# Filler matmuls ahead of and behind the PV of heads 25 to 27, and the tail rows in other loads

## The chip, the cores and the metric

The kernel runs on one core of a Trainium2 chip. The metric is device time in microseconds, from the start to the end of one execution; each run is one execution, and the median over runs is compared. All data are float32.

## What is computed

One decode step for a batch of 2, with one query position. The input x (2 x 512) is normalised over its 512 features, and the result goes to two branches that are added to x:

```
xn  = layernorm(x)                             # no scale, no shift
q   = xn @ wq                                  # 32 heads of 128
p   = softmax(q . k[:, :, -2048:] / sqrt(128)) # per head, over the last 2048 cached positions
att = (p @ v[:, :, -2048:]) @ wo               # 32 * 128 -> 512
glu = ((xn @ w_gate) * (xn @ w_up)) @ w_down   # 512 -> 1376 -> 512, no nonlinearity
y   = x + att + glu
```

Keys and values of the window are 2 x 32 x 2048 x 128 floats each, 134 MB of the 159.57 MB that are loaded. Each of them is used once.

## The kernel before

The inputs are laid out anew beforehand as one long `stream`, in the order in which they are used, so that a load of `n` columns is 128 rows of `n` consecutive floats. `blocks` lists the loads and the fields in each; `packed` fills loads of 15872 columns (7936 KB). There are three such buffers, the tiles named `step`. `pump` issues the next load on SyncE's queue (SP) when the last field of a buffer has been used (`done`); SP takes its issues in order.

For a head h the work is this. `products` (VectorE) multiplies the keys by the query in place, `sums` adds over the 128 features, `maxima` takes the maximum (with a reduction over the partitions on GpSimd), `weights` the exponentials (ScalarE) and their sum, `reciprocals` one over the sum. `pv` multiplies the weights by the values on TensorE into a PSUM tile `o_ps` and copies it out on ScalarE; `transpose` turns the result into columns `oT`, scaled by the reciprocals; `project_o` multiplies by the head's rows of wo and adds into `acc`. The order on TensorE, VectorE, ScalarE and SP is the order in which the program is written (`InOrder`).

A head's PV is eight matmuls (`weigh`), each of 16 stationary columns and 512 moving ones. A float32 matmul stands in the trace as two instructions, called halves below. PV runs some heads behind the products. After head 28's step the ends are written out by hand: products of heads 28, 29 and 30, then PV of heads 25 to 27 (`pv([H - 7]), pv([H - 6, H - 5])`), their transposes and output projections, PV of 28, and so on to head 31. Between these stand filler matmuls, `keep_busy(n)`: they multiply a constant by n columns of `spare_in` into a PSUM tile `spare` that nothing reads.

The values of head 25 lie in two loads: the first half (four matmuls) with the keys of heads 28 and 29, the second half with the keys of 30 and the values of 26 and 27. The next load holds the keys of 31, the values of 28 and two blocks of w_down.

The last 96 rows of w_down (1376 = 10 * 128 + 96) don't fill a block of 128. 46 of them lie, beside x itself, in the field `wr` of the stream; the last 50 lie as 25 rows of two side by side in `tail`, and are loaded into rows 28 to 52 of the tile `wd_tail`, five rows at a time, behind the first four loads. The rows of `wd_tail` below 28 are zero. `down_rest` multiplies both by the GLU's hidden values (`hX`), early on, at head 3.

## Time and profile before

| | |
|---|---|
| median of 3 runs | 379.49 us (379.06 to 384.83) |
| the profiled execution | 379.92 us, span 378.1 us |
| TensorE, VectorE, ScalarE busy | 257.4, 295.4, 57.2 us |
| loaded from HBM | 159.50 MB, 422 GB/s over the span |
| DMA queue of SP | 97.8% of 16 engines' span |

The span runs from the first to the last instruction of the profiled execution; its time is 1.8 us longer. The times in rows of the trace are microseconds from the span's start. All instructions of the wrapped engines stand under line 126, the wrapper's, so rows are told apart by tiles: `o_ps` is PV, `tr` the transposes, `acc` the output projections and w_down, and `q` is the queries' projection or, late in the program, the fillers, whose tile comes from the same pool.

### The profile page before, as it was taken

The numbers are of one execution on the slowest core, as the hardware profiler recorded it, in microseconds if no ns is written. First come the engines' busy times: TensorE is split into PE (matmuls) and PEld (weight loads), VectorE is DVE, ScalarE is ACT, GpSimd is POOL, SyncE is SP. The second block draws the span as 40 slices with busy tenths as digits, with TensorE's granted clock in tenths as the row PEclk, the third lists the DMA queues.
The fourth block names the chain that finished last, engine by engine and source line by source line (L and its number), as shares of the span: only waits on it lengthen the run. The fifth ranks groups of instructions, "written<-read, shape, count | busy, mean of one in ns | idle before, by whom it ended". The sixth has DMA issues, their size and how long they took to land.

```text
span 378.1 us, 2875 instructions
## 1 busy us (share of the span) xinstructions
PE 257.4 (68%) x1096; PEld 88.2 (23%) x1096; DVE 295.4 (78%) x145; ACT 57.2 (15%) x260; POOL 25.2 (7%) x74
## 2 busy tenths in 40 slices
PE   3166796886587880776668806895647774738996
PEld 3132123222222220222123202331212221202343
DVE  4069998369979479999179999892899999999550
ACT  1002011110211210021012002111101110202131
POOL 1000000000001000000000000000000000000010
PEclk9999696798576896598958865889567888666999
DMA  8999999999999999999999999999999999999993
GB/s 341 435 488 436 416 404 434 437 430 432 431 437 430 430 430 432 450 437 430 443 432 431 430 430 437 437 426 437 430 430 430 432 443 430 437 426 417 420 424 121
DMA packets 3950, 159.73 MB, mean 422 GB/s; under 512 B 457, under 2 KB 713, under 8 KB 994
## 3 DMA queue, kind: packets, MB, share of 16 engines
q1 hardware_dynamic: 3938, 159.57, 97.8%
q8 instruction: 8, 0.13, 0.1%
q14 instruction: 4, 0.03, 0.0%
HBM read 159.50 MB, written 0.07 MB: 422 GB/s over the span
## 4 chain that ended last, share of the span: by engine, by line
DMA 61%; DVE 19%; PE 17%; ACT 1%; issue 0%; SPq 0%; DVEq 0%
DMA step<-in_stream_dram 61%; DVE s L126 9%; DVE step L126 9%; PE o_ps L126 6%; PE acc L126 4%; PE q L126 4%; PE tr L126 3%; ACT o_sb L126 1%; ACT oT L126 0%; DVE m L126 0%; SPq L126 0%; DVE o_out L126 0%; DVE rec L126 0%; DVEq L126 0%
## 5 line engine op out<-in xcount | busy, mean ns | idle before, releaser
L126 DVE TENSOR_TENSOR step<-step,q 128x4096 f32<-128x4096 f32 x31 | 136.8, 4412 | 45.8 <-DMA step<-in_stream_dram 42.0
L126 DVE TENSOR_REDUCE s<-step 128x32 f32<-128x4096 f32 x32 | 141.4, 4419 | 1.1
L126 PE MATMUL o_ps<-step,p 128*16 128x512 f32 x512 | 81.5, 693 | 50.0 <-DMA step<-in_stream_dram 49.9
L126 PE MATMUL q<-step,xnb 128*128 128x512 f32 (+1 forms) x128 | 77.2, 754 | 31.7 <-DMA step<-in_stream_dram 31.7
L126 PEld LDWEIGHTS q<-step,xnb 128*128 128x128 f32 x128 | 29.5, 246 | 83.2 <-issue 67.8
L126 PE MATMUL acc<-step,oT 128*2 128x512 f32 (+1 forms) x88 | 38.3, 597 | 8.5 <-ACT oT L126 8.5
L126 PE MATMUL tr<-first,o_sb 128*128 128x2 f32 (+4 forms) x192 | 29.8, 274 | 15.7 <-ACT o_sb L126 11.8
L126 PEld LDWEIGHTS o_ps<-step,p 128*16 128x16 f32 x512 | 14.3, 103 | 106.1 <-DMA step<-in_stream_dram 58.6
L126 PEld LDWEIGHTS tr<-first,o_sb 128*128 128x128 f32 (+2 forms) x192 | 27.1, 216 | 40.4 <-ACT o_sb L126 34.3
L126 ACT COPY o_sb<-o_ps 128x512 f32<-128x512 f32 x23 | 13.5, 585 | 150.2 <-PE o_ps L126 150.2
L321 POOL PARTITION_ALL_REDUCE mm<-m x32 | 11.4, 357 | 241.1 <-DVE rec L126 136.0
L126 ACT ACTIVATE nm<-mm 128x2 f32<-128x2 f32 x32 | 6.6, 205 | 126.7 <-POOL mm L321 126.7
L337 POOL PARTITION_ALL_REDUCE sum<-rs x32 | 12.7, 398 | 99.9 <-ACT p L126 99.9
L126 ACT ACTIVATE p<-s,nm 128x16 f32<-128x16 f32 x64 | 19.2, 300 | 1.0
L126 PE MATMUL o_ps<-step,xn 128*2 128x512 f32 (+1 forms) x48 | 14.9, 682 | 5.9 <-DMA step<-in_stream_dram 5.9
L126 ACT ACTIVATE oT<-tr,rec 128x1 f32<-128x1 f32 x64 | 12.1, 260 | 27.7 <-PE tr L126 27.7
L126 DVE TENSOR_TENSOR step<-step,tr 128x4096 f32<-128x4096 f32 x1 | 4.4, 4422 | 15.0 <-DMA step<-in_stream_dram 15.0
L126 ACT ACTIVATION_READ_ACCUMULATOR p<-s,nm 128x1 f32 x64 | 11.9, 187 | 0.0
L126 PEld LDWEIGHTS acc<-step,oT 128*2 128x2 f32 x88 | 4.3, 88 | 21.8 <-ACT oT L126 12.2
L126 DVE RECIPROCAL rec<-sum 128x2 f32<-128x2 f32 x32 | 5.0, 155 | 4.2 <-POOL sum L337 4.2
L126 PE MATMUL q<-xnb,mean_w 128*128 128x512 f32 (+4 forms) x20 | 7.4, 461 | 0.0
L126 PE MATMUL acc<-step,hT 128*2 128x128 f32 (+2 forms) x72 | 7.1, 310 | 0.0
(40 smaller groups left out, 39.2 us busy)
## 6 DMA issues: line engine op xcount, KB each, us to landing
step<-in_stream_dram SPq DMA_DIRECT2D x15, 7936.0 KB, 31.8
step<-in_stream_dram SPq DMA_DIRECT2D x1, 7808.0 KB, 38.8
step<-in_stream_dram SPq DMA_DIRECT2D x1, 7680.0 KB, 20.9
step<-in_stream_dram SPq DMA_DIRECT2D x1, 7552.0 KB, 57.9
step<-in_stream_dram SPq DMA_DIRECT2D x1, 4864.0 KB
step<-in_stream_dram SPq DMA_DIRECT2D x1, 3328.0 KB, 20.0
step<-in_stream_dram SPq DMA_DIRECT2D x1, 2304.0 KB, 25.0
step<-in_stream_dram SPq DMA_DIRECT2D x2, 1024.0 KB, 14.2
```

Of the source, the lines that this page charges most:

```text
L126: made = call(*args, **kwargs)
L321: nc.gpsimd.partition_all_reduce(mm, m, P, bass_isa.ReduceOp.max)
L337: nc.gpsimd.partition_all_reduce(sum_t[h], rs, P, bass_isa.ReduceOp.add)
```

## The change

It has three parts. First, three matmuls of 512 columns go ahead of the PV of heads 25 to 27. Like the other fillers they write `spare`; their moving operand is head 29's keys after `products` has multiplied them. They stand in the program between `products` and `sums` of head 29. Second, the one filler of 512 columns behind the output projections of 25 to 27 becomes three, of 512, 512 and 256. Third, the 25 rows of `tail` come in one load, and the last four of the 46 rows leave `wr` for a new input `edge`; they are loaded one by one into rows 24 to 27 of `wd_tail`, first 512 columns. The stream keeps its size: `wr` holds zeros where they were.

```diff
-NT, FT, FP, TS = 2, 25, 28, 5
+NT, FT, FP, TS = 2, 25, 28, 4
...
-    for i in range(0, FT, FT // TS):
-        sp.dma_start(wd_tail[FP + i : FP + i + FT // TS, :], tail[i : i + FT // TS, :])
+    sp.dma_start(wd_tail[FP : FP + FT, :], tail)
+    for i in range(TS):
+        sp.dma_start(wd_tail[FP - TS + i : FP - TS + i + 1, :D], edge[i : i + 1, :])
...
+    spare = ps_q.tile([P, B, GC], F32, name="q")[:, 0, :]
     for h in (H - 4, H - 3):
         products(h)
+        if h == H - 3:
+            for i in range(3):
+                pe.matmul(
+                    spare, mean_w, got["k", h][0][:, i * FB : (i + 1) * FB], start=True, stop=True
+                )
         sums(h)
         maxima(h)
         weights(h)
         reciprocals(h - 1)
 
     h = H - 2
-    spare = ps_q.tile([P, B, GC], F32, name="q")[:, 0, :]
     products(h)
     sums(h)
     o_sbs = pv([H - 7]), pv([H - 6, H - 5])
...
     for i in range(H - 7, HF):
         project_o(i)
-    keep_busy(GC)
+    for n in (GC, GC, 256):
+        keep_busy(n)
...
-    mixed[:, :RX] = np.concatenate([a, rest[:FX]]).reshape(RX, 2, HD).swapaxes(0, 1)
+    whole = np.concatenate([a, rest[: FX - TS]])
+    mixed[:, : RX - TS] = whole.reshape(RX - TS, 2, HD).swapaxes(0, 1)
...
         "tail": rest[FX:].reshape(NT, FT, D).swapaxes(0, 1).reshape(FT, NT * D),
+        "edge": rest[FX - TS : FX],
```

TensorE's program at the new fillers, between the output projections of heads 23 and 24 (`acc`) and PV of head 25 (`o_ps_93` with the weights `p_97`) and head 26 (`o_ps_92`, `p_98`):

```order
 L126 MATMUL acc<-step,oT_111 2x512
 L126 MATMUL acc<-step,oT_108 2x512
+L126 MATMUL q<-step,mean_w 128x512 x3
 L126 MATMUL o_ps_93<-step,p_97 16x512 x8
 L126 MATMUL o_ps_92<-step,p_98 16x512 x8
```

All eight matmuls of head 25, of both halves of its values, now stand behind the three fillers.

TensorE's program between the output projections of 26 and 27 and PV of head 28 (`p_100`), which two blocks of w_down (`hT`) follow:

```order
 L126 MATMUL acc<-step,oT_110 2x512
 L126 MATMUL acc<-step,oT_111 2x512
-L126 MATMUL q<-xnb,mean_w 128x512
+L126 MATMUL q<-xnb,mean_w 128x512 x2
+L126 MATMUL q<-xnb,mean_w 128x256
 L126 MATMUL o_ps_93<-step,p_100 16x512 x8
 L126 MATMUL acc<-step,hT 2x512 x2
```

One filler has become two of its size and one of half.

SP's queue at the start of the program:

```order
 L126 DMA step<-in_stream_dram 128x15104
-L126 DMA wd_tail<-in_tail_dram 5x1024 x5
+L126 DMA wd_tail<-in_tail_dram 25x1024
+L126 DMA wd_tail<-in_edge_dram 1x512 x4
 L126 DMA step<-in_stream_dram 128x15872 x15
 L126 DMA step<-in_stream_dram 128x9728
```

Five small issues stay five, at the same place behind the first three large loads.

## The prediction

> **What bounds the kernel now.** First the page: span, engines, DMA, and the chain that ended last.

> ```profile
> span 378.1 us, 2875 instructions
> PE 257.4 (68%) x1096; PEld 88.2 (23%) x1096; DVE 295.4 (78%) x145; ACT 57.2 (15%) x260; POOL 25.2 (7%) x74
> q1 hardware_dynamic: 3938, 159.57, 97.8%
> DMA 61%; DVE 19%; PE 17%; ACT 1%; issue 0%; SPq 0%; DVEq 0%
> ```

> The loads fill the 16 DMA engines for 97.8% of the span, so up to the last loads the kernel runs at the pace of its stream. The edit on TensorE sits at the end of that stream, so the chain in order of time comes next (start, length, what).

> ```profile
> 303.27 37.99 DMA step<-in_stream_dram
> ...
> 341.31 7.20 PE o_ps L126 x40
> 348.51 1.00 PE tr L126 x8
> ...
> 351.05 0.54 PE q L126 x2
> 351.58 2.67 PE acc L126 x6
> 354.25 1.06 PE q L126 x2
> 355.31 1.84 PE o_ps L126 x16
> ...
> 362.83 1.84 PE o_ps L126 x16
> ...
> 366.76 0.98 PE o_ps L126 x8
> ...
> 368.38 1.84 PE o_ps L126 x16
> 370.21 0.52 PE q L126 x2
> 370.74 1.02 PE o_ps L126 x8
> ...
> 373.48 1.92 PE acc L126 x80
> ```

> From 341.31 to 375.4 us the chain is TensorE's own program, one piece after the other. It starts when the load with the values of heads 26 and 27 lands, and no later load stands in it. The page's list of issues says how far behind the loads are (KB, median us to landing), and the queue's timeline when the first was issued:

> ```profile
> step<-in_stream_dram SPq DMA_DIRECT2D x1, 3328.0 KB, 20.0
> step<-in_stream_dram SPq DMA_DIRECT2D x1, 2304.0 KB, 25.0
> 340.65 15.38 SPq L126 DMA_DIRECT2D step<-in_stream_dram  x6
> ```

> Issued at 340.65, the 3328 KB (values of head 29) land at 360.7, and PV of 29 starts at 362.83: 2.2 us of slack. The 2304 KB (values of 30), issued right behind, land at 366 and are used at 368.38. So the end moves one for one with TensorE, earlier by at most some 2 us, later without limit.

> Last the granted clock (the column after POOL) in stretches of 3.41 us, which fall on the steps of the clock:

> ```profile
> 329.76:333.17 3.41, 3.41 (x11) 0.57 (x10) 3.38 (x4) 0.83 (x5) 0.35 (x1) 0.50 0.99 428
> 333.17:336.58 3.41, 0.69 (x2) 0.00 (x0) 3.38 (x2) 0.06 (x1) 0.40 (x1) 1.00 1.07 465
> 336.58:340.00 3.42, 0.00 (x0) 0.00 (x0) 3.42 (x1) 0.00 (x0) 0.00 (x0) 0.50 0.83 359
> 340.00:343.41 3.41, 2.10 (x12) 0.48 (x16) 2.97 (x4) 1.03 (x6) 0.75 (x2) 0.50 1.03 445
> 343.41:346.82 3.41, 3.41 (x20) 0.67 (x16) 3.38 (x2) 0.45 (x1) 0.00 (x0) 0.50 0.95 411
> 346.82:350.24 3.42, 2.92 (x27) 1.43 (x19) 3.38 (x2) 1.00 (x3) 0.00 (x0) 1.00 1.01 430
> ```

> A stretch in which PE was busy throughout (3.41) is followed by clock 1.00; one with 2.10 or less is followed by 0.50. So 5.5 of the 7.2 us of PV of 25 to 27 run at half clock. That is what the new fillers go for.

> **The change, part by part.** *Fillers ahead.* TensorE takes its instructions in order, and what stands at this place before is:

> ```profile
> 330.80 1.90 PE L126 MATMUL o_ps<-step,p 128*16 128x512 f32 x6
> 332.50 1.36 PE L126 MATMUL o_ps<-step,p 128*16 128x512 f32 x2
> 331.74 4.40 DVE L126 TENSOR_TENSOR step<-step,q 128x4096 f32<-128x4096 f32 x1
> 336.17 4.42 DVE L126 TENSOR_REDUCE s<-step 128x32 f32<-128x4096 f32 x1
> ```

> The eight halves at 330.80 to 333.86 are the first four matmuls of head 25, whose first half of values is there early (an f32 matmul stands as two instructions). They run in idle time today. The fillers stand ahead of them and read head 29's products, which VectorE ends at 336.1. So those eight are now queued behind the fillers: the path gets 3 fillers and 8 halves in front of the 40.

> What a 512 wide matmul with 128 stationary columns takes cold is bounded by the first row, two of them; warm it is the chain's 1.06:

> ```profile
> 153.71 3.75 PE L126 MATMUL q<-step,xnb 128*128 128x512 f32 x4 [11.71 <-DMA step<-in_stream_dram]
> ```

> That is 1.88 cold. With this execution's clock steps: the fillers start at 336.2 on a cold clock, since the work that raised it at 333.17 (the eight halves) no longer stands there. 336.2 to 340.0 holds 3.8 / 1.88 = 2.02 of them. The stretch from 336.58 to 340.00 is then full, so the clock rises at 340.0, and the other 0.98 take 1.04: fillers done at 341.04, just before the load lands. Eight warm halves (the 0.98 of 366.76) end at 342.0, forty (2.5 times the 1.84 of sixteen) at 346.6. Before, the forty ended at 348.51: **1.9 us gained**, and without a rise of the clock there is no gain at all.

> The steps may lie elsewhere against the program in another execution. The earliest rise is 3.41 after 336.2, at 339.6: 1.81 fillers by then, 1.19 x 1.06 more, 0.98 and 4.6 end at 346.4. The latest, where the fillers just miss a step and need the next whole stretch, is 336.2 + 2 x 3.41 = 343.0: all fillers cold (5.64, to 341.84), 1.16 us of the eight at half speed, 0.4 more, 4.6: 348.0. So the gain is between 0.5 and 2.1 against this execution.

> [...]

> *Fillers behind.* One of 512 columns becomes two of 512 and one of 256. 512 cost 1.06 (354.25) and 256 cost 0.54 (351.05), all warm: **1.60 us added**, between the output projections of 25 to 27 and PV of 28. Does a wait cover them? PV of 28 needs the load with head 31's keys; VectorE shows when that comes:

> ```profile
> 352.82 4.42 DVE L126 TENSOR_TENSOR step<-step,q 128x4096 f32<-128x4096 f32 x1 [2.37 <-DMA step<-in_stream_dram]
> 358.95 0.68 DVE L126 COPY o_sb<-acc 2x512 f32<-2x512 f32 x1 [1.71 <-PE acc L126]
> ```

> It lands at 352.8. The projections, 1.9 earlier, end at 352.35; PV of 28 could start at 352.8 without any filler. The fillers (1.06 + 1.06 + 0.54 = 2.66) push it to 355.0 instead of 355.31. So of the 1.9 about 0.3 stays: **the sum is 378.1 - 0.3 = 377.8 of span**. VectorE's copy of the accumulator waits for TensorE (1.71 idle), so it and the sums of head 31 behind it move along with PE; below that idle time VectorE gives no new bound. Over the clock's positions the net is 1.6 - 2.1 = -0.5 to 1.6 - 0.5 = +1.1.

> *The late load.* Head 29's keys and the first half of 25's values share a buffer (they stand in one load). Its next load was issued at 340.65 when the sums of 29 ended; now it waits for the eight halves at 342.0, at most 343.4. It queues behind the load that lands at 352.8, so 10 us cover it. Cost nothing; without that cover 1.4.

> *The tail rows.* Five loads of 5 rows become one of 25, then four of one 2 KB row; five issues stay five:

> ```profile
> wd_tail<-in_tail_dram SPq DMA_DIRECT2D x5, 20.0 KB
> DMA packets 91, 1.69 MB, mean 483 GB/s; under 512 B 41, under 2 KB 41, under 8 KB 66
> ```

> The second row is the DMA view of 57 to 60.5 us: 25 packets of 4 KB (66 - 41), amid a stream that keeps its rate. The same 25 rows move; new are 8 KB. At one engine's share of the page's 422 GB/s (26.4) they are 0.3 us if one engine takes them all. Below nothing is possible too, since one completion takes the place of five, 0.3 the other way. The far bound is a row that costs a whole small transfer, issue to landing, each in turn; the store at the end is the nearest:

> ```profile
> SPq L675 <- DMA out_dram<-o_out: 0.9, 1, 0.9
> 375.74 0.35 SPq L126 DMA_DIRECT2D out_dram<-o_out  x1
> ```

> 0.35 + 0.9 = 1.3, four of them 5 us. I take 0.3, nearest to how the 25 packets ran, and it costs nothing: TensorE now reaches the second half of head 25 at 342.0, 0.7 after its load, PV of 28 stands 2.2 after its own.

> [...] The packets' count agrees with whole rows; which engine takes them no row here shows.

> Against the median: the profiled execution took 379.92, the median of the runs shown is 379.49. 379.92 - 0.3 is 379.6 for the same clock steps; the middle of -0.5 and +1.1 is +0.3, 380.2. Brought to the median (0.43 lower) these are 379.2 and 379.8. **I forecast 379.5 us, no change.**

> **The rivals.**

> *The fillers don't raise the clock before 346.8* (slower). Place: PV of 25 to 27. Price: fillers to 341.84, then 48 halves, 5.6 warm; 5.0 us at half speed do 2.5, the other 3.1 end at 349.9. That is 1.4 late, and 1.6 of fillers behind: +3.0, 382.5 from the median. The net turns into a loss from a rise at 340.7 on (PV of 27 done at 346.9, 1.6 earlier); this case begins past 343.0, the latest rise that full stretches allow. For it: the stretch with 2.10 busy raised nothing, so a gap would do. Against: the fillers and the eight halves leave no gap.

> *The clock is still high when the fillers start* (faster). Then they take 3.2, to 339.4, the eight halves run before the landing, and the forty end at 345.9: 2.6 - 1.6 = 1.0 gained, 378.5. Against: 0.69 busy in 333.17:336.58 let it fall, and there is less there now.

> *The single rows hold one engine for 5 us.* Every load behind is late by it: PV of 26 starts at 346.3 instead of about 342, so the end is some 4 us late, 383.4. Against: 25 packets took their place amid the stream.

> **How the numbers follow.** Forecast 0.74, slow clock 0.12, warm start 0.06, single rows 0.04; 0.04 for what I don't see. The range is 378.4 to 381.6: from the warm start to the late rise with the runs' own scatter of 0.4, and part of the way to the slow clock. About 2% (7.6 us) is what a measurement of this kernel can tell from no change. No case reaches it: faster 0.02, within 0.94, slower 0.04.

> **What would show it.** Three fillers from 336.2 for 4.6 to 5.7 us, clock 1.00 by 343.0 instead of 346.8, PV of 25 to 27 done between 346.4 and 348.0, PV of 28 within 1 us of 355.3, and the queue's late issue at 342 with no hole in the stream. The forecast is wrong if PV of 28 waits for its load behind the fillers, if the clock stays at 0.50 to 346, or if the chain from 350 on holds a DMA step.

## The result, and the profile after

The changed kernel takes 379.19 us (median of 14 runs, 378.06 to 380.18), the kernel before 379.37 in the 14 runs beside it. The ratio is 1.0001, interval 0.999 to 1.0012: no change, as forecast. Executions more than 1.5% above the fastest of their kernel, such as the one of 384.83 us, are left out of this ratio and of those below. The profiled execution took 379.05 us, its span is 377.2.

The chain in order of time (start, length, what), at the place of the edit:

```profile
335.55 5.46 PE q L126 x6
341.01 5.33 PE o_ps L126 x48
346.34 1.00 PE tr L126 x8
...
349.42 2.67 PE acc L126 x6
352.08 2.35 PE q L126 x6
354.43 1.84 PE o_ps L126 x16
...
361.95 1.84 PE o_ps L126 x16
...
372.60 1.92 PE acc L126 x80
```

Three fillers (six halves), then 48 halves of PV where 40 stood, ended at 346.34 instead of 348.51. Behind the projections three fillers stand in 2.35 us where one stood in 1.06. The granted clock (column after POOL), on this execution's steps:

```profile
334.28:337.69 3.41, 2.14 (x3) 1.14 (x4) 3.38 (x2) 0.00 (x0) 0.00 (x0) 0.50 1.03 447
337.69:341.11 3.42, 3.42 (x8) 0.86 (x11) 2.99 (x4) 0.44 (x3) 0.36 (x1) 0.50 0.74 317
341.11:344.52 3.41, 3.41 (x36) 0.83 (x32) 3.41 (x1) 1.04 (x5) 0.40 (x1) 1.00 1.19 514
344.52:347.93 3.41, 2.91 (x29) 1.33 (x21) 3.38 (x2) 1.00 (x3) 0.00 (x0) 1.00 0.90 381
```

The first stretch that the fillers fill is 337.69 to 341.11, and the clock rises at 341.11, as PV starts (341.01). VectorE and the queue of loads:

```profile
340.54 4.42 DVE L126 TENSOR_TENSOR step<-step,q 128x4096 f32<-128x4096 f32 x1 [0.39 <-DMA step<-in_stream_dram]
342.12 0.81 SPq L126 DMA_DIRECT2D step<-in_stream_dram  x2
```

The first row is the product of head 30, which starts as the load with the values of 26 and 27 lands: 340.5, against 341.3 before. The second is the late load, issued at 342.12 behind the eight halves instead of at 340.65; it lands 17.7 us later, at 359.9, where before it was 360.6, and PV of 29 starts behind that, at 361.95. PV of 28 starts 0.88 earlier than before in this pair of profiles. Some 0.7 of it goes with the stream, which is early here: the load above by 0.75, and the products of head 29, which the fillers wait for, by 0.74 (331.00 against 331.74).

### The profile page after: what moved, and what is told of

It reads as the page before. It is cut to its first block, busy times and chain, and to the rows that moved or that the text cites. A ratio compares the mean times of both kernels' runs of the same rounds, so it can differ in the third digit from the quotient of the medians.

```text
span 377.2 us, 2895 instructions
## 1 busy us (share of the span) xinstructions
PE 257.0 (68%) x1106; PEld 89.0 (24%) x1106; DVE 295.4 (78%) x145; ACT 57.4 (15%) x260; POOL 25.3 (7%) x74
## 2 busy tenths in 40 slices
DMA packets 3938, 159.74 MB, mean 423 GB/s; under 512 B 441, under 2 KB 697, under 8 KB 982
## 4 chain that ended last, share of the span: by engine, by line
DMA 60%; PE 20%; DVE 18%; ACT 1%; issue 1%; SPq 0%; DVEq 0%
DMA step<-in_stream_dram 60%; DVE step L126 9%; DVE s L126 8%; PE q L126 7%; PE o_ps L126 6%; PE acc L126 4%; PE tr L126 3%; ACT o_sb L126 1%; ACT oT L126 0%; DVE m L126 0%; SPq L126 0%; DVE o_out L126 0%; DVE rec L126 0%; DVEq L126 0%
## 5 line engine op out<-in xcount | busy, mean ns | idle before, releaser
L126 DVE TENSOR_TENSOR step<-step,q 128x4096 f32<-128x4096 f32 x31 | 136.8, 4412 | 44.3 <-DMA step<-in_stream_dram 38.4
L126 DVE TENSOR_REDUCE s<-step 128x32 f32<-128x4096 f32 x32 | 141.4, 4419 | 1.1
L126 PE MATMUL o_ps<-step,p 128*16 128x512 f32 x512 | 77.3, 663 | 42.7 <-DMA step<-in_stream_dram 42.7
L126 PE MATMUL q<-step,xnb 128*128 128x512 f32 (+1 forms) x128 | 76.2, 742 | 33.6 <-DMA step<-in_stream_dram 33.6
L126 PEld LDWEIGHTS q<-step,xnb 128*128 128x128 f32 x128 | 28.9, 242 | 84.1 <-issue 68.6
L126 PE MATMUL acc<-step,oT 128*2 128x512 f32 (+1 forms) x88 | 36.3, 572 | 8.6 <-ACT oT L126 8.6
L126 PE MATMUL tr<-first,o_sb 128*128 128x2 f32 (+4 forms) x192 | 29.3, 271 | 16.9 <-ACT o_sb L126 11.8
L126 PEld LDWEIGHTS tr<-first,o_sb 128*128 128x128 f32 (+2 forms) x192 | 26.7, 213 | 42.4 <-ACT o_sb L126 35.2
L126 ACT COPY o_sb<-o_ps 128x512 f32<-128x512 f32 x23 | 13.5, 586 | 149.3 <-PE o_ps L126 149.3
L126 PEld LDWEIGHTS o_ps<-step,p 128*16 128x16 f32 x512 | 13.6, 100 | 95.3 <-DMA step<-in_stream_dram 50.1
L126 ACT ACTIVATE nm<-mm 128x2 f32<-128x2 f32 x32 | 6.6, 205 | 125.9 <-POOL mm L323 125.9
L126 ACT ACTIVATE p<-s,nm 128x16 f32<-128x16 f32 x64 | 19.2, 300 | 1.0
L126 PE MATMUL o_ps<-step,xn 128*2 128x512 f32 (+1 forms) x48 | 13.7, 630 | 5.4 <-DMA step<-in_stream_dram 5.4
L126 ACT ACTIVATE oT<-tr,rec 128x1 f32<-128x1 f32 x64 | 12.1, 260 | 27.7 <-PE tr L126 27.7
L126 DVE TENSOR_TENSOR step<-step,tr 128x4096 f32<-128x4096 f32 x1 | 4.4, 4421 | 15.0 <-DMA step<-in_stream_dram 15.0
L126 ACT ACTIVATION_READ_ACCUMULATOR p<-s,nm 128x1 f32 x64 | 11.9, 186 | 0.0
L126 PEld LDWEIGHTS acc<-step,oT 128*2 128x2 f32 x88 | 4.2, 86 | 20.7 <-ACT oT L126 12.1
L126 DVE RECIPROCAL rec<-sum 128x2 f32<-128x2 f32 x32 | 5.0, 155 | 4.9 <-POOL sum L339 4.9
L126 PE MATMUL q<-xnb,mean_w 128*128 128x512 f32 (+4 forms) x24 | 8.7, 465 | 0.0
L126 PE MATMUL q<-step,mean_w 128*128 128x512 f32 x6 | 5.5, 1083 | 4.3 <-DVE step L126 4.3
## 6 DMA issues: line engine op xcount, KB each, us to landing
step<-in_stream_dram SPq DMA_DIRECT2D x1, 3328.0 KB, 17.7
step<-in_stream_dram SPq DMA_DIRECT2D x1, 2304.0 KB, 22.8
```

Of the source, the lines that this page charges most:

```text
L126: made = call(*args, **kwargs)
```

## The experiments

Differences in microseconds below are a ratio times 379.4; the interval stands behind. None of them reaches 2%; they are read from the intervals, over 5 to 12 executions of each kernel. Each profile shows one execution, and the executions differ, as will be seen; the medians decide.

**Fillers ahead alone.** The first part of the change in the kernel before, nothing else.

> The kernel before with the three fillers ahead of PV of 25 to 27 alone; one filler of 512 behind and the tail loads as before. Theory (the fillers ahead raise the clock and shorten PV, the fillers behind give it back, the loads do nothing): PV of 25 to 27 ends 1.4 to 1.9 us sooner after its load, nothing gives that back, PV of 28 starts at 353.4 to 353.9 instead of 355.3, and the median is 1.3 us lower than before (0.5 to 2.1 over the positions of the clock's steps). Rival 1 (the end is set by the stream, so nothing on TensorE counts here): within 0.3 of before. Rival 2 (the single-row loads are what changed the trace): within 0.3 of before.

Measured: 378.22, ratio 0.9965 (0.9948 to 0.9981), so 1.3 us lower (0.7 to 2.0). Its profiled execution was the slowest of its twelve, and shows one way in which they differ. The chain:

```profile
336.38 4.34 PE q L126 x6
340.72 5.27 PE o_ps L126 x48
...
349.07 4.36 PE acc L126 x6
353.43 1.06 PE q L126 x2
354.49 1.84 PE o_ps L126 x16
```

PV ends at 345.99, 2.5 earlier than before, though its load landed at about the same time (341.4): more than the 1.4 to 1.9 expected. But then the projections take 4.36 instead of 2.67: the clock has fallen again behind the transposes, and PV of 28 starts at 354.49, later than the 353.4 to 353.9 expected. More on that below. The clock's stretches show the early rise and the fall:

```profile
336.04:339.46 3.42, 3.08 (x4) 1.50 (x5) 3.39 (x2) 0.00 (x0) 0.00 (x0) 0.50 0.89 384
339.46:342.87 3.41, 3.41 (x27) 0.85 (x29) 2.98 (x4) 1.14 (x6) 0.67 (x2) 1.00 0.95 411
...
346.29:349.70 3.41, 2.91 (x19) 1.96 (x19) 3.41 (x1) 1.48 (x7) 0.00 (x0) 1.00 0.96 411
349.70:353.11 3.41, 3.41 (x5) 0.39 (x3) 1.00 (x4) 0.00 (x0) 0.35 (x1) 0.50 0.95 411
```

The fillers had 3.08 of the first stretch, not the whole, and the clock rose behind it.

**Fillers behind alone.**

```diff
-    keep_busy(GC)
+    for n in (GC, GC, 256):
+        keep_busy(n)
```

> The kernel before with the fillers behind alone (512, 512 and 256 instead of 512). Theory: they lie on the path that sets the end, so the median is 1.3 to 1.6 us higher than before, with PV of 25 to 27 at half clock as before. Rival 1 (the stream sets the end): within 0.3 of before.

Measured: 380.59, ratio 1.0025 (1.0007 to 1.0043), 0.9 us higher (0.3 to 1.6). The two halves of the change on TensorE are real, of opposite sign and of about one size. The rival that the stream sets the end (within 0.3 of before) falls with the fillers ahead; this run's interval only just reaches it.

**Tail loads alone.** The third part of the change, no filler added.

> The kernel before with the new tail loads alone. Theory: within 0.3 us of before, and the landing of the load with the values of 26 and 27 moves by less than 0.4 in either direction beyond what executions differ by. Rival 2 (the loads even out the 16 engines, which is why the whole stream stood 0.74 us earlier in the changed kernel's profile): the landing at 340.5 instead of 341.3, and the median 0.7 lower.

Measured: 379.13, ratio 0.9984 (0.9968 to 1.0), 0.6 lower (0 to 1.2). In the profile the load with the values of 26 and 27 lands early, as in the changed kernel:

```profile
340.64 4.42 DVE L126 TENSOR_TENSOR step<-step,q 128x4096 f32<-128x4096 f32 x1 [0.41 <-DMA step<-in_stream_dram]
```

So the expectation on the landing was wrong and the one on the time is not settled by this run.

**One filler ahead.** `range(3)` of the first run becomes `range(1)`.

> The kernel before with one filler ahead instead of three, nothing else. Theory (the clock rises only after a whole stretch of 3.41 us of work): the filler and the eight halves run cold from 336.2 to 340, then PE waits for the load at 341.3, no stretch before it is full, PV of 25 to 27 runs cold as before and takes 5.5 to 7.4 us from the landing: within 0.4 us of before. Rival 3 (every filler gives its share, whatever the stretches): a third of the gain of three, 0.4 to 0.5 lower than before.

Measured: 378.59, ratio 0.9971 (0.9951 to 0.9991), 1.1 us lower (0.3 to 1.9). The theory expected nothing; the rival a third. In the profiled execution the filler indeed raised nothing:

```profile
334.74:338.15 3.41, 2.07 (x6) 0.60 (x10) 3.38 (x2) 0.00 (x0) 0.00 (x0) 0.50 1.03 447
338.15:341.56 3.41, 2.23 (x12) 0.20 (x16) 2.93 (x4) 0.36 (x2) 0.35 (x1) 0.50 0.90 387
341.56:344.98 3.42, 3.42 (x20) 0.68 (x16) 3.42 (x1) 1.11 (x5) 0.40 (x1) 0.50 1.00 432
344.98:348.39 3.41, 3.41 (x32) 1.38 (x24) 3.38 (x2) 0.58 (x1) 0.00 (x0) 1.00 1.00 427
```

But four of its twelve runs stand at 377.67 to 377.86, lower than every run of the kernel before beside them (378.23 and up). My expectation had counted the filler as 1.9 us. With the eight halves behind it, it is work from 336.08 to 339.97 without a break, 3.9 us, into which a stretch of 3.41 fits in some executions, and more often still the 3.08 that sufficed above. No profile was taken of one of the four, so this is argued so far. It makes a prediction: one filler that stands behind the eight halves, and so alone, must give nothing.

**One filler, alone.** The eight halves first (below), then one filler on the products.

> One filler on head 29's products, behind the first four matmuls of head 25: TensorE works from 336.1 to 338.1 and then waits for the load at 341.2. With one filler ahead of those four (the run before of one filler) the work went on from 336.1 to 340.0, 3.9 us, so that a clock stretch of 3.41 fits into it in some executions. Theory (the clock rises after a stretch busy nearly throughout; that is where the 0.85 of the one filler came from): here none fits, PV of 25 to 27 runs as before, median within 0.3 of before. Rival 3 (a filler gives its share by itself): 0.4 to 0.9 lower than before, as with one filler ahead.

Measured: 379.33, ratio 0.9995 (0.9984 to 1.0006). That is 0.2 us lower (-0.6 to +0.2), as the theory says; the rival's 0.4 to 0.9 lies outside the interval but for its lower end. In the profile the clock rises at 345.46 only, behind a stretch that PV itself fills. A filler by itself is worth little or nothing; what counts, by these runs, is how much of one stretch is work.

**Seven early fillers.** The first four matmuls of head 25 stay ahead, and seven fillers on constants, which wait for nothing on VectorE, fill the idle time behind them.

```diff
+        if h == H - 3:
+            part = H - 7, 0, 4
+            weigh(H - 7, got["v", part][0], range(4), True, False)
+            done("v", part)
+            for _ in range(7):
+                keep_busy(GC)
```

> The kernel before with seven fillers of 512 on constants ahead, behind the first four matmuls of head 25, so that they wait for nothing on VectorE and fill TensorE's idle time from 332.8 to the load at 341.2; nothing else. Theory (the clock rises after a whole busy stretch): in every execution it is high when the load lands, wherever its steps fall; PV of 25 to 27 takes 4.6 us from the landing instead of 6.3 to 7.2, ends at 345.8, and the median is 1.7 to 2.1 us lower than before, more than with the three fillers on the products (1.2). Rival 3 (any work ahead gives a gain by its order, not by the clock): no better than with three, 1.2 or less. Rival 4 (the loads behind allow no more): PV of 28 waits for its load and the gain stays at 1.2.

Measured: 378.17, ratio 0.9955 (0.9939 to 0.9971), 1.7 us lower (1.1 to 2.3). PV runs at full clock from its first instruction. The chain and the clock's stretches:

```profile
340.87 4.49 PE o_ps L126 x40
...
348.43 4.36 PE acc L126 x6
```

```profile
338.74:342.16 3.42, 1.72 (x13) 0.36 (x16) 2.98 (x4) 1.07 (x6) 0.50 (x2) 1.00 0.90 387
342.16:345.57 3.41, 3.41 (x35) 0.99 (x27) 3.38 (x2) 0.56 (x2) 0.26 (x1) 1.00 0.92 399
345.57:348.98 3.41, 2.91 (x19) 2.04 (x20) 3.41 (x1) 1.56 (x7) 0.00 (x0) 1.00 1.13 484
348.98:352.39 3.41, 3.41 (x5) 0.39 (x3) 1.00 (x3) 0.00 (x0) 0.35 (x1) 0.50 0.86 371
```

The 4.49 is 1.6 to 2.7 less than any PV that started cold. The rivals' 1.2 is still in the interval; against rival 3 speaks the clock in these rows, against rival 4 that PV of 28 follows TensorE's own work here. Of the gain 1.7 is lost to the projections: the stretch from 345.57 holds nearly all of the sixteen halves of the transposes (2.04 in the weight loads, third column), and the clock falls behind it. The changed kernel's stretch from 344.52 has the same 2.91 of busy PE but 1.33 of weight loads, and the clock stays.

**The 25 rows in one load, nothing else.** No single rows; the last four rows stay in `wr`.

> The kernel before with the 25 tail rows in one load; no single rows, no fillers added. All executions with five tail loads had the load with the values of 26 and 27 at 341.1 to 341.3, both with one load and four single rows at 340.5 to 340.7. Theory A (it is the five loads taken into one): landing at 340.4 to 340.7, median 0.3 to 0.6 lower than before. Theory B (the single rows do it, by evening out the engines): landing at 341.1 to 341.3, median within 0.2 of before.

Measured: 379.58, ratio 0.9998 (0.9983 to 1.0013). The landing was at 340.68, as theory A says, and the time did not move, as theory B says. The two belong apart: the landing moves, the time does so by less than either run can tell. The DMA view of 57 to 60.5 us shows what the merged load saves, here and with the single rows:

```profile
DMA packets 73, 1.81 MB, mean 518 GB/s; under 512 B 21, under 2 KB 21, under 8 KB 46
```

```profile
DMA packets 80, 1.76 MB, mean 503 GB/s; under 512 B 25, under 2 KB 25, under 8 KB 54
```

The first is the merged load alone, the second the changed kernel. Of the smallest packets, under 512 B, 41 stand there before and 21 with the merged load alone, so 20 fewer, and 25 in the changed kernel.

**Three fillers behind the eight halves.** As the first run, with the four matmuls of head 25 ahead of the fillers.

> The kernel before with the three fillers on head 29's products, but behind the first four matmuls of head 25 instead of ahead of them; nothing else. Theory: these four are off the path again, so PV of 25 to 27 ends 0.4 to 1.0 us sooner than with the fillers ahead of them, and the median is 1.5 to 2.0 lower than before (1.2 with them ahead). Rival (their place does not count, since they fill the wait for the load): 1.2 lower, as with them ahead.

Measured: 378.0, ratio 0.9961 (0.9946 to 0.9976), 1.5 lower (0.9 to 2.0), against 1.3: the place of the eight halves is not told apart by the time. The profiled execution, one of the faster ones, shows a limit. TensorE's timeline, with the idle time before a piece in brackets:

```profile
336.22 4.51 PE L126 MATMUL q<-step,mean_w 128*128 128x512 f32 x6 [2.35 <-DVE step L126]
341.23 4.49 PE L126 MATMUL o_ps<-step,p 128*16 128x512 f32 x40 [0.50 <-DMA step<-in_stream_dram]
...
352.71 1.91 PE L126 MATMUL o_ps<-step,p 128*16 128x512 f32 x16 [0.19 <-DMA step<-in_stream_dram]
...
360.58 1.91 PE L126 MATMUL o_ps<-step,p 128*16 128x512 f32 x16 [0.28 <-DMA step<-in_stream_dram]
```

PV of 28 and of 29 now wait for their loads. TensorE has caught up with the stream, 2.2 us ahead of where it was at head 29.

**All together.** Seven early fillers, no filler behind the projections, the merged load.

> Seven fillers on constants ahead, behind the first four matmuls of head 25; no filler behind the projections of 25 to 27; the 25 tail rows in one load. Theory: PV of 28 starts when its load lands (352.0 to 352.7) instead of at 355.3, the later loads then leave about 2.2 us, and the median is 2.2 to 3.0 lower than before. Rival (without the filler behind the clock falls again, or the later loads end the gain): 1.7 to 2.1 lower, as with the fillers behind kept.

Measured: 377.67 (377.44 to 377.92), ratio 0.9944 (0.9928 to 0.9959), 2.1 lower (1.6 to 2.7). It is the lowest time so far, though theory (2.2 to 3.0) and rival (1.7 to 2.1) both lie in the interval. All its five runs lie within 0.5 us, where those of the kernel before spread over 1.6 and more. The timeline:

```profile
340.70 4.49 PE L126 MATMUL o_ps<-step,p 128*16 128x512 f32 x40 [1.73 <-DMA step<-in_stream_dram]
...
348.20 4.43 PE L126 MATMUL acc<-step,oT 128*2 128x512 f32 x6
352.19 2.16 PE L126 MATMUL o_ps<-step,p 128*16 128x512 f32 x16
...
360.06 1.91 PE L126 MATMUL o_ps<-step,p 128*16 128x512 f32 x16
```

PV of 28 starts at 352.19, within the 352.0 to 352.7 that the theory has for its load, and the clock still falls at the transposes, as the rival says. The next two runs ask whether that costs anything here.

**A filler between the transposes**, in the run of seven early fillers and in the one of all together:

```diff
     transpose([H - 7], o_sbs[0], 1 - bank)
+    keep_busy(GC)
     transpose([H - 6, H - 5], o_sbs[1])
```

> The run with seven early fillers, with one more filler of 512 between the transposes of head 25 and those of 26 and 27, where TensorE waits 0.5 us for ScalarE. In that run's profile the clock fell at 349.0, behind a stretch that holds the transposes, and the projections took 4.36 instead of 2.67. Theory (the early gain is partly lost there: the transposes count as little work for the clock): with the filler the clock stays, the projections take 2.67 in the profile, and the median is 0.3 to 0.8 lower than the 1.5 below before of that run. Rival 4 (the loads cap the gain): PV of 28 and 29 wait for their loads, and the median is 2.0 below before at most. Rival (the filler costs its own 0.6 and keeps nothing): 0.9 to 1.5 below before.

> Seven early fillers behind the first four matmuls of head 25, none behind the projections, one tail load, and the filler between the transposes. Theory (the loads cap the gain at some 2 us): the projections take 2.67, PV of 28 and of 29 start when their loads land, and the median is 2.0 to 2.4 below before, hardly better than without that filler (2.0). Rival (TensorE still sets the end): 2.6 or more below before.

Measured: the first 0.9972 (0.9954 to 0.999), 1.1 lower (0.4 to 1.8), no better than the 1.7 of the run without that filler; the two intervals overlap, and it decides nothing. The second 377.65, 0.9952 (0.994 to 0.9964), 1.8 lower (1.4 to 2.3), no better than without. Its timeline shows both readings at once:

```profile
348.38 2.74 PE L126 MATMUL acc<-step,oT 128*2 128x512 f32 x6
352.16 1.91 PE L126 MATMUL o_ps<-step,p 128*16 128x512 f32 x16 [1.04 <-DMA step<-in_stream_dram]
...
360.03 1.91 PE L126 MATMUL o_ps<-step,p 128*16 128x512 f32 x16 [0.28 <-DMA step<-in_stream_dram]
```

The projections are back at 2.7 us, and what they save turns into a wait of 1.04 for the load of 28. PV of 28 starts at 352.16 against 352.19. So TensorE has nothing more to give here: from about 2 us on the stream sets the end.

## Why the prediction was right, and where not

*The clock decides PV.* Right, and more closely than the prediction had it. The profiles of the runs in which PV of 25 to 27 started cold give its start, the rise of the clock and its length:

| run | start | rise | length | 4.49 + half of (rise - start) |
|---|---|---|---|---|
| before | 341.31 | 346.82 | 7.20 | 7.25 |
| fillers behind alone | 341.13 | 344.78 | 6.27 | 6.32 |
| tail loads alone | 340.66 | 344.25 | 6.24 | 6.29 |
| one filler ahead | 341.15 | 344.98 | 6.36 | 6.41 |
| merged load alone | 340.70 | - | 6.48 | - |
| one filler, alone | 342.12 | 345.46 | 6.12 | 6.16 |

4.49 is the length at full clock (seven early fillers, above), and each cold microsecond cost half of one; for the merged load alone no view shows the rise. That the steps of the clock lie elsewhere against the program in another execution, which the prediction took up without a trace that shows it, is seen here: the rises stand at 344.25 to 346.82, 3.3 to 5.5 behind the start of PV. In the changed kernel the clock rose 5.6 behind the start of the first filler (335.55 to 341.11), with the fillers ahead alone 3.1 behind it (336.38 to 339.46).

*Fillers ahead.* The fillers started at 335.55, 0.65 sooner than in the sum. On the sum's axis, with that added, the clock rose at 341.8 (340.0 in the sum, bounds 339.6 to 343.0) and PV was done at 347.0, within its 346.4 to 348.0. The near bound itself was too late: it asked for a whole stretch, 3.41 us of fillers, and in the run of the fillers ahead alone the clock rose after 3.08. There 48 halves took 5.27, where the sum had 5.6, and PV was done at 345.8 on the same axis. The gain was 1.3 in the medians; the sum had 1.9 for one execution and 0.5 to 2.1 over all. What the sum did not know is that the profiled execution before had the latest rise of the five in the table, 5.5 after the start of PV where the others have 3.3 to 3.8. A usual PV before lasts some 6.3, so a usual gain is smaller.

*Fillers behind.* 1.60 was the sum, 2.35 - 1.06 = 1.29 the profile, 0.9 (0.3 to 1.6) the median. The sum took 1.06 for each filler of 512, the length of one between other work; three in a row took 2.35, or 0.94 for each 512 columns.

*The net.* -0.3 was predicted for the same steps, no change for the median; 0.0 (-0.4 to +0.5) was measured, and the parts (-1.3, +0.9, -0.6 to -0.1) add up to it within their intervals. That the forecast came so near is in part luck: in the profiles the fillers ahead gave some 1.5 instead of 1.9, the fillers behind cost 1.29 instead of 1.60, and the two misses cancel.

*The late load and the end.* It was issued at 342.12 (342 predicted), and no load behind it came later than before. The end moved with TensorE, and the bound of some 2 us that the slack of 2.2 before PV of 29 gave is where PV of 29 came to wait for its load, 0.28 in the profiles of two runs (1.5 and 1.8 gained); in that of a third (2.1 gained) it starts without a wait, at 360.06 against their 360.58 and 360.03.

*The tail rows.* The term "0.3, costs nothing" had the wrong sign for the stream: the load with the values of 26 and 27 landed at 340.5 to 340.7 in all five profiles with one load of 25 rows, and at 340.9 to 341.4 in six of the seven with five (the execution of 383.4 us, a profile of the run with a filler between the transposes, is not among them). In the seventh, at 342.1, the stream was 0.8 late from its first load on. A gain, of 0.3, stood in the prediction as possible. In time it is 0 to 1.2 with the single rows and -0.5 to 0.6 without. That it counts for little fits the table, since an earlier start buys half-clock time alone; that is argued, not shown. Why five loads for one should move the whole stream by some 0.5 us stays open. The starts of VectorE's products show where it comes in. At 49 us they lie at 49.32 to 49.57 in the profiles with one load and at 49.26 to 49.56 in six of those with five (the seventh is the late stream, at 50.22). At 60, where the tail rows' packets run, two with one load have 59.60 and 59.80 and four with five have 59.65 to 60.49, so the two groups still overlap. At 322 they are apart: 321.92 to 322.05 against 322.21 to 322.75 in the six.

On which engines the rows run no view here shows, nor that a single row holds one. What the DMA view of 57 to 60.5 us counts is that the four single rows add 4 packets under 512 B (25 - 21).

*The rivals.* None came. A clock raised late would have shown a PV of 48 halves near 8 us; it took 5.33. A clock still high would have shown fillers of 3.2 us; they took 5.46. Single rows that hold an engine for 5 us would have shown late loads; they landed early.

## What to carry to other kernels

A filler that warms TensorE was worth little here until work covered most of one stretch of the clock (2.79 of 3.41 us, see below), and the stretch lay elsewhere in every profile (rises 3.3 to 5.5 us behind the start of PV): give the filler nothing to wait for, make the work long enough for any position, and read several profiles before sizing the gain. Count what is queued behind the filler and what the filler's companions give back: here -1.3 and +0.9 were parts of one edit. Before tuning an engine at the end of a load-bound kernel, read from the loads' landings how far the end can move at all.

## What was not expected of the hardware

In three profiles the clock fell behind a stretch in which TensorE shows 2.91 of 3.41 us busy, when the transposes' weight loads took 1.96 to 2.08 of it; in the changed kernel it stayed with the same 2.91 and 1.33 of weight loads. With the filler between the transposes it stayed too, at 3.41 busy. And with seven early fillers it stayed behind a stretch with 1.72 busy only (338.74, shown above).

```profile
172.75:176.16 3.41, 2.79 (x12) 0.33 (x4) 3.41 (x1) 0.58 (x1) 0.00 (x0) 0.50 0.86 372
176.16:179.57 3.41, 2.85 (x12) 1.54 (x13) 3.38 (x2) 1.20 (x8) 0.40 (x1) 1.00 1.07 465
39.63:43.04 3.41, 2.55 (x8) 0.39 (x10) 3.38 (x4) 0.90 (x5) 0.75 (x2) 0.50 1.06 461
43.04:46.45 3.41, 3.41 (x12) 0.53 (x10) 3.38 (x2) 0.00 (x0) 0.00 (x0) 0.50 0.98 425
```

```profile
313.80:317.22 3.42, 1.32 (x14) 0.11 (x3) 3.38 (x2) 0.00 (x0) 0.40 (x1) 1.00 1.11 483
317.22:320.63 3.41, 0.00 (x0) 0.00 (x0) 3.41 (x1) 0.00 (x0) 0.00 (x0) 0.50 0.95 410
132.90:136.31 3.41, 1.56 (x12) 0.34 (x12) 1.58 (x1) 0.00 (x0) 0.00 (x0) 1.00 0.90 391
136.31:139.72 3.41, 2.22 (x12) 1.05 (x10) 3.38 (x2) 1.00 (x3) 0.00 (x0) 1.00 1.03 447
```

The 59 stretches with transposes don't keep to these edges. At half clock 15 of 16 stayed low, with up to 2.91 busy; at full clock 18 of 43 fell, with up to 2.49. Without the time of the transposes themselves the 15 have 2.32 at most and the 18 have 1.44 at most, while the one that rose has 3.10 and the 25 that stayed high have 1.47 or more. So in these two profiles the clock went as if the transposes by matmul (128 wide weight loads but for a few, 2 to 6 moving columns) were no work. That they are the cause is the author's reading of these counts; no run was made to test it or the edges.
